# Two weight preparations in a fused FFT and gated MLP: first blocks taken in groups, projections in one PSUM bank each

## The chip, the cores and the metric

The kernel runs on one core of a Trainium2 chip. The metric is the device time of one execution in microseconds (us); lower is better. PE is TensorE (PEld its weight loads), DVE VectorE, ACT ScalarE, POOL GpSimd, SP the engine that only issues transfers.

## The reference

```
X = fft(x, axis=1); X = fft(X, axis=2).real      # x: 4 x 3008 x 256
h = X.reshape(12032, 256) @ w_in                 # 256 x 2048
g = h / (1 + exp(-h))
out = g @ w_out                                  # 2048 x 256, 12032 rows
```

[...]

## The kernel before

**What is computed where.** The transform over the 256 columns is folded into `w_in`: a cosine and sine table (`dft_sb`) is multiplied with each block of `w_in`, and the product is the left operand of the first layer. The transform over the 3008 rows is a matmul of folded rows of `x` with tables (`t2`, `te`, `to`). Its result is cut into 16 chunks (four classes in each of four batches) of about 376 columns. Each chunk runs against 16 blocks of 128 hidden columns, so the main loop has 256 steps (c, f). Every product is made from high and low parts in `float32r` (`uvh` and `uvl`, `abh` and `abl`, `gh` and `gl`, `woh` and `wol`), three matmuls for one.

**A step.** `first(c, f)` issues 6 matmuls of the first layer into a tile `pq` (two buffers of two PSUM banks). `act` lets DVE add a rank-one row (`ub` times `a128`, L349) and form sum and difference (L353, L354), then ACT makes Silu into `h` (L360) and the high part `gh` (L361). `rest` of the step before lets DVE subtract for the low part `gl` (L369). `second` of three steps earlier (LAG = 3) issues 12 matmuls into four accumulators `acc` (L380, L381, L385). In chunk 0 the first DIRECT = 8 steps take another way: 12 matmuls with a negated copy `vneg` give sum and difference at once (L332), there is no DVE work between PE and Silu, and the row `a128` and `ub` aren't needed.

**The beginning.** `w_in` comes in eight blocks of 256 columns. `load_w` loads one (SP, three buffers `win`), `ahead` starts `to_f32` with an absolute value on ACT (L76), `run(conv.pop(q))` finishes it with four DVE operations (L78, L80, L82, L84) into `wf` (two buffers), `project` multiplies with the table on PE (L441), `large` takes row 0 out on ACT (`row`, L446), sends it through a transfer to `a128` (L447, issued by ACT) and makes `abh` (L450), and `small` makes `abl` on DVE (L454). The projection has a tile of two banks, from a pool `ps` of two buffers, for blocks 1 and 3 from `pq`. Blocks 0 to 3 are done ahead of the main loop, between the folding of the first rows of `x` (`first_sums`, L167 to L173, once for 64 rows of `x2` and once for 128 rows of `x1`), the operand of chunk 0 (L213 to L220, `xh` L251, `xl` L264), its transform on PE (L280) and `spread`, which makes `row`, `ub` (a transfer, L312), `uvh`, `uvl` and `vneg`. Blocks 4 to 7 are finished inside steps 0, 1 and 2 (`late_w`, L513). The rows of `x` come as a load by SP and a second load by POOL that adds to it (L134).

**The second weight.** `w_out` comes in eight blocks too, two loaded by POOL at the start, the others by SP (L95) when the block two earlier has been read. `convert_all_wo` is a generator with four pulls a block: the same conversion, then `woh` on ACT (L101) and `wol` on POOL (L102). `act` pulls it in chunk 0: three times a step in the direct steps, once in the others.

**What sets the order.** Nothing reorders: each engine executes its instructions as the code emits them. Buffers are rings: a tile of a tag waits until the readers of the tile that held the buffer are done. The tag `half` has three buffers, shared by `row`, the `wf` of `w_out`, and parts of the folding. After step 2 the pools `wr` and `ps` are closed, and their place goes to the accumulators and the tables `te` and `to`.

## Time and profile before

| | before |
|---|---|
| median of 3 runs | 944.23 us (944.03 to 945.05) |
| profiled execution, its own time | 944.83 us |
| span of the profiled execution | 942.9 us |
| mean granted clock of PE | 0.975 |
| busy: PE, DVE, ACT, POOL | 887.7, 748.0, 534.3, 183.9 us |

The span is what lies between the first and the last instruction in the trace; the execution's own time is 1.9 us longer. A granted clock of 1.00 is 2.4 GHz, 0.50 is 1.2 GHz. Busy time of PE is modelled from pipelined matmuls, so a window in which PE is busy throughout says that it never waited long, and the count of matmuls in it says how fast it went.

### The profile page before, as it was taken

What the parts mean: (1) busy time and instruction counts of PE and PEld (TensorE: products, weight loads), DVE (VectorE), ACT (ScalarE), POOL (GpSimd) and SP (SyncE); (2) the same over time, 40 slices, a digit from 0 to 9 for tenths busy, and PEclk for the clock granted to TensorE, in tenths of its full rate; (3) what the DMA queues carried; (4) which work ended last, traced back from release to release, by engine and by line L of the source; (5) the groups of instructions that cost most, each with busy time, mean ns of one, the idle gap of its engine ahead of it and who ended that gap; (6) DMA issues with size and microseconds to landing.
All of it is one profiled execution on the core that took longest, in us unless ns stands there. A gap on an engine that the chain in (4) does not pass through costs nothing.

```text
span 942.9 us, 12965 instructions
## 1 busy us (share of the span) xinstructions
PE 887.7 (94%) x5056; PEld 879.2 (93%) x5056; DVE 748.0 (79%) x1199; ACT 534.3 (57%) x736; POOL 183.9 (20%) x212
## 2 busy tenths in 40 slices
PE   2455999999999999999999999999999999999998
PEld 1344999999999999999999999999999999999998
DVE  4534888799787979798887979798887978798785
ACT  1332657665556756475564646475654646465554
POOL 1000415329013205236030105230010101010000
PEclk8766999999999999999999999999999999999999
DMA  9510251160302027020302024020302020020300
GB/s 283 104 53 31 90 107 56 20 134 1 42 1 9 34 19 201 3 40 1 42 1 9 33 21 111 3 40 1 42 1 9 33 9 34 4 39 1 43 1 33
DMA packets 19453, 40.96 MB, mean 43 GB/s; under 512 B 3264, under 2 KB 13504, under 8 KB 17472
## 3 DMA queue, kind: packets, MB, share of 16 engines
q1 hardware_dynamic: 16352, 28.87, 16.6%
q0 software_dynamic: 1600, 10.81, 4.8%
q10 hardware_dynamic: 1440, 0.46, 0.8%
q8 instruction: 39, 0.64, 0.3%
q14 instruction: 22, 0.18, 0.1%
HBM read 24.70 MB, written 12.34 MB: 39 GB/s over the span
## 4 chain that ended last, share of the span: by engine, by line
PE 87%; DVE 6%; ACT 3%; DMA 1%; issue 1%; ACTq 0%; POOL 0%; DVEq 0%
PE acc L385 18%; PE acc L381 18%; PE acc L380 18%; PE pq L336 9%; PE pq L337 9%; PE pq L338 8%; PE pq L280 5%; PE pw L441 2%; PE pq L332 2%; DMA raw<-in_x_dram 1%; DVE gl L369 1%; DVE wf L84 1%; DVE wf L82 1%; PE pq L441 1%; ACT h L360 1%
## 5 line engine op out<-in xcount | busy, mean ns | idle before, releaser
L360 ACT ACTIVATE h<-h 128x752 f32<-128x752 f32 (+2 forms) x250 | 207.3, 829 | 290.9 <-DVE h L354 288.4
L381 PE MATMUL acc<-gh,wol 128*128 128x376 f32 (+1 forms) x1024 | 342.8, 335 | 0.0
L380 PE MATMUL acc<-gh,woh 128*128 128x376 f32 (+1 forms) x1024 | 342.3, 334 | 0.0
L369 DVE TENSOR_TENSOR gl<-h,gh 128x752 fp32r<-128x752 f32 (+2 forms) x258 | 254.9, 988 | 3.5 <-ACT gh L361 3.3
L385 PE MATMUL acc<-gl,woh 128*128 128x376 f32 (+1 forms) x1024 | 226.3, 335 | 0.0
L361 ACT ACTIVATE gh<-h 128x752 fp32r<-128x752 f32 (+2 forms) x258 | 214.2, 830 | 8.2
L349 DVE SCALAR_TENSOR_TENSOR h<-ub,a,pq 128x376 f32<-128x376 f32 (+1 forms) x248 | 150.0, 605 | 56.7 <-PE pq L338 54.8
L381 PEld LDWEIGHTS acc<-gh,wol 128*128 128x128 f32 x1024 | 192.7, 188 | 0.0
L380 PEld LDWEIGHTS acc<-gh,woh 128*128 128x128 f32 x1024 | 192.5, 188 | 0.0
L385 PEld LDWEIGHTS acc<-gl,woh 128*128 128x128 f32 x1024 | 181.2, 189 | 0.0
L336 PE MATMUL pq<-uvh,abh 128*128 128x376 f32 (+1 forms) x496 | 166.6, 336 | 0.0
L337 PE MATMUL pq<-uvl,abh 128*128 128x376 f32 (+1 forms) x496 | 166.2, 335 | 0.0
L338 PE MATMUL pq<-uvh,abl 128*128 128x376 f32 (+1 forms) x496 | 166.0, 335 | 0.0
L354 DVE TENSOR_TENSOR h<-h,pq 128x376 f32<-128x376 f32 (+1 forms) x248 | 135.7, 547 | 8.5
L353 DVE TENSOR_TENSOR h<-h,pq 128x376 f32<-128x376 f32 (+1 forms) x248 | 135.6, 547 | 8.3
L258 POOL TENSOR_TENSOR xl<-xf,xh 128x256 fp32r<-128x256 f32 x53 | 49.1, 950 | 382.0 <-ACT xh L251 190.9
L338 PEld LDWEIGHTS pq<-uvh,abl 128*128 128x128 f32 x496 | 93.6, 189 | 0.0
L337 PEld LDWEIGHTS pq<-uvl,abh 128*128 128x128 f32 x496 | 93.5, 189 | 0.0
L336 PEld LDWEIGHTS pq<-uvh,abh 128*128 128x128 f32 x496 | 93.4, 188 | 0.1
L441 PE MATMUL pw<-wf,dft_sb 128*128 128x256 f32 x48 | 22.2, 644 | 43.1 <-DVE wf L84 43.1
L441 PEld LDWEIGHTS pw<-wf,dft_sb 128*128 128x128 f32 x48 | 15.1, 329 | 48.3 <-DVE wf L84 29.5
L314 DVE TENSOR_TENSOR uvl<-pq,uvh 128x752 fp32r<-128x752 f32 (+1 forms) x16 | 15.1, 943 | 55.4 <-ACT uvh L313 55.4
(99 smaller groups left out, 541.4 us busy)
## 6 DMA issues: line engine op xcount, KB each, us to landing
out_dram<-o SPq DMA_DIRECT2D x48, 188.0 KB, 2.2
raw<-in_x_dram SPq DMA_DIRECT2D x5, 1024.0 KB, 11.4
raw<-in_x_dram POOLq DMA_DIRECT2D x5, 1024.0 KB, 8.1
win<-in_w_in_dram SPq DMA_DIRECT2D x8, 512.0 KB, 7.9
wo<-in_w_out_dram SPq DMA_DIRECT2D x6, 512.0 KB, 3.6
out_dram<-o SPq DMA_DIRECT2D x16, 189.0 KB, 2.2
ub<-row SPq DMA_DIRECT2D x11, 188.0 KB, 8.5
t<-in_t_dram POOLq DMA_DIRECT2D x1, 1128.0 KB, 13.5
```

The costliest lines, as they stand in the source:

```text
L336: nc.tensor.matmul(po, abh[:, i, fs], uvh[:, i, :n], start=True, stop=False)
L337: nc.tensor.matmul(po, abh[:, i, fs], uvl[:, i, :n], start=False, stop=False)
L338: nc.tensor.matmul(po, abl[:, i, fs], uvh[:, i, :n], start=False, stop=True)
L349: stt(p[:, :n], ub[:, :n], a128[f // 2][:, f % 2:f % 2 + 1], pq[:, 0, :n], op0=ALU.mult, op1=ALU.add)
L353: tt(h[:, 0, :n], p[:, :n], pq[:, 1, :n], op=ALU.add)
L354: tt(h[:, 1, :n], p[:, :n], pq[:, 1, :n], op=ALU.subtract)
L360: nc.scalar.activation(h[:, sg, :n], (pq if direct else h)[:, sg, :n], AF.Silu)
L361: nc.scalar.activation(gh[:, sg, :n], h[:, sg, :n], AF.Copy)
L369: tt(gl[:, sg, :n], g[:, sg, :n], gh[:, sg, :n].bitcast(F32), op=ALU.subtract)
L380: nc.tensor.matmul(po, wo[0][f // 2][:, f % 2, es], gh[:, sg, :n], start=f == 0, stop=False)
L381: nc.tensor.matmul(po, wo[1][f // 2][:, f % 2, es], gh[:, sg, :n], start=False, stop=False)
L385: nc.tensor.matmul(accs[c][i][:, :n], wo[0][f // 2][:, f % 2, es], gl[:, sg, :n], start=False, stop=f == NF - 1)
```

## The change

- **The order at the beginning.** Blocks 0, 1 and 2 of `w_in` are started one after the other (`ahead`, then `convert`, which is the rest of the conversion and the projection) before the first folding; blocks 5 and 6 likewise, around the transform. Blocks 0 to 6 are projected before step 0. Only `large(6)`, `project(7)` (step 0), `small(6)`, `large(7)` and `small(7)` (step 1) remain in the loop. `late_w` is gone, and the pools are closed after step 1.
- **Buffers.** A projection has a tile of one bank (two halves of 256 columns), four buffers in `ps`, none from `pq`. `win` has five buffers in place of three. `wf` of `w_in` comes from the ring `half` of three buffers, which `row` of `spread` and the `wf` of `w_out` share. The row for `a128` has a place of its own for each block (`rows`) in place of a buffer of `half`.
- **Queues.** The transfers to `a128` and the first `ub` are issued by SP, no longer by ACT. The load of `w_in` block 0 goes ahead of the rows of `x`, and blocks 1 and 2 go ahead of the 128 rows of `x1`.
- **Direct steps.** 6 in place of 8, so block 3 gets the extra ACT copy that zeroes its row 0, and the tables `te` and `to` are loaded at step 6.
- **`w_out`.** Loads run three blocks ahead in place of two; every third block has a buffer in the pool `tabs`. The absolute value of a block is emitted between the second and third DVE operation of the block before. The pulls are 2 in steps 0 and 1, 3 in steps 2 to 4, 2 in steps 5 to 15.
- **Later.** In chunk 1 the operand of chunk 2 is queued at step 8 in place of 10, and POOL's budget there is 1.3 in place of 1.1.

```diff
-DIRECT = 8
+DIRECT = 6
 def load_wo(q, queue=nc.sync):
-        wo_raw[q] = fold_p.tile([128, 2, D], I64, tag="ri0", name="wo", bufs=2)
+        wo_raw[q] = (tabs_p.tile([128, 2, D], I64, tag="wo", name="wo") if q % 3 == 2 else
+                     fold_p.tile([128, 2, D], I64, tag="ri0", name="wo", bufs=2))
 def convert_all_wo():
         for q in range(NF // 2):
+            for _ in range(2):
+                next(work)
+                yield
+            if q + 1 < NF // 2:
+                following = convert_wo(q + 1)
+                next(following)
             yield from work
-            if q + 2 < NF // 2:
-                load_wo(q + 2)
-            if q + 1 < NF // 2:
-                work = convert_wo(q + 1)
-                next(work)
+            if q + 3 < NF // 2:
+                load_wo(q + 3)
+            work = following
             yield
 def spread(c, po):
-        (nc.sync if c else nc.scalar).dma_start(out=ub[:, :n], in_=...)
+        nc.sync.dma_start(out=ub[:, :n], in_=...)
-    ps = late.enter_context(tc.tile_pool(name="ps", bufs=2, space=PSUM))
+    ps = late.enter_context(tc.tile_pool(name="ps", bufs=4, space=PSUM))
+    rows = wr.tile([128, 2, 128, 2], F32, name="rows")
 def load_w(q):
-        win[q] = wr.tile([128, 2, 256], I64, tag="win", name="win", bufs=3)
+        win[q] = wr.tile([128, 2, 256], I64, tag="win", name="win", bufs=5)
 def ahead(q):
-        wf32[q] = wr.tile([128, 2, 256], F32, tag="wf", name="wf", bufs=2)
+        wf32[q] = fold_p.tile([128, 2, 256], F32, tag="half", name="wf", bufs=3)
 def project(q):
-        pw = pws[q] = pq_tile() if q in (1, 3) else ps.tile([128, 2, 512], F32, tag="ps", name="pw")
+        pw = pws[q] = ps.tile([128, 2, 256], F32, tag="ps", name="pw")
 def large(q):
-        row = fold_p.tile([1, 128, 2], F32, tag="half", name="row", bufs=3)
+        row = rows[32 * (q % 4):32 * (q % 4) + 1, q // 4]
-        nc.scalar.dma_start(out=a128[q], in_=row)
+        nc.sync.dma_start(out=a128[q], in_=row)
...
+    load_w(0)
     load_x(1, 0, lo)
-    load_w(0)
+    load_w(1)
+    load_w(2)
     load_x(0, 0)
...
+    def convert(q):
+        run(conv.pop(q))
+        project(q)
     ahead(0)
+    ahead(1)
+    convert(0)
+    ahead(2)
+    convert(1)
     large(0)
+    convert(2)
+    ahead(3)
+    large(1)
+    small(0)
     run(first_sums(1, lo))
+    small(1)
+    large(2)
+    convert(3)
+    ahead(4)
+    small(2)
     run(first_sums(0))
...
+    large(3)
+    ahead(5)
+    ahead(6)
+    convert(4)
+    small(3)
     run(op)
     po = pq_tile()
+    run(conv.pop(5))
     transform(0, po)
+    project(5)
+    large(4)
+    convert(6)
     spread(0, po)
+    ahead(7)
+    small(4)
+    large(5)
+    run(conv.pop(7))
+    small(5)
...
+        if n == 0:
+            large(6)
+            project(7)
+        elif n == 1:
+            small(6)
+            large(7)
...
-            act(c, f, (3 if f < DIRECT else 1) * (wo_work,) if c == 0 else ())
-        if n < LAG:
-            for q in ((4, 5), (6,), (7,))[n]:
-                late_w(q)
-        if n == LAG - 1:
+            act(c, f, (2 + (1 < f < 5)) * (wo_work,) if c == 0 else ())
+        if n == 1:
+            small(7)
             late.close()
...
+            load_wo(2)
```

Three places of the built order follow, each before and then after. First DVE at the very beginning, from its fifth instruction on (the four before it are the conversion of block 0 in both). Before:

```order
L167 TENSOR_TENSOR raw<-raw 64x8x127
L169 SCALAR_TENSOR_TENSOR raw<-raw 64x8x127
L171 TENSOR_TENSOR sm<-raw 64x4x129
L173 TENSOR_TENSOR sm<-raw 64x4x127
L454 TENSOR_TENSOR abl<-pw,abh 128x2x256
L78 TENSOR_SCALAR wf<-wf 128x512
```

After:

```order
L78 TENSOR_SCALAR wf<-wf 128x512
L80 TENSOR_SCALAR wf<-wf 128x512
L82 SCALAR_TENSOR_TENSOR wf<-win,wf 128x512
L84 SCALAR_TENSOR_TENSOR wf<-win,wf 128x512
L78 TENSOR_SCALAR wf<-wf 128x512
L80 TENSOR_SCALAR wf<-wf 128x512
L82 SCALAR_TENSOR_TENSOR wf<-win,wf 128x512
L84 SCALAR_TENSOR_TENSOR wf<-win,wf 128x512
L460 TENSOR_TENSOR abl<-pw,abh 128x2x256
L172 TENSOR_TENSOR raw<-raw 64x8x127
```

Blocks 1 and 2 of `w_in` moved ahead of `abl` of block 0 and of the folding. The second place is ACT around the first Silu (`h<-pq`). Before:

```order
L450 ACTIVATE abh<-pq 128x2x256
L76 ACTIVATE wf<-wo 128x512
L360 ACTIVATE h<-pq 128x2x376
L361 ACTIVATE gh<-h 128x2x376
L446 ACTIVATE row<-pw 1x256
L447 DMA a_4_81<-row 128x1x2
L449 ACTIVATE pw<-zero 1x256
L450 ACTIVATE abh<-pw 128x2x256
L76 ACTIVATE wf<-win 128x512
```

After:

```order
L452 ACTIVATE rows<-pw 1x256
L455 ACTIVATE pw<-zero 1x256
L456 ACTIVATE abh<-pw 128x2x256
L76 ACTIVATE wf<-wo 128x512
L365 ACTIVATE h<-pq 128x2x376
L366 ACTIVATE gh<-h 128x2x376
L452 ACTIVATE rows<-pw 1x256
L455 ACTIVATE pw<-zero 1x256
L456 ACTIVATE abh<-pw 128x2x256
```

The absolute value of `w_out` block 0 stands ahead of the first Silu in both; around it stand blocks 3 and 4 of `w_in` before, and blocks 6 and 7 after. The third place is DVE in two steps of chunk 0 that are no longer direct. Before:

```order
L369 TENSOR_TENSOR gl<-h,gh 128x2x376
L349 SCALAR_TENSOR_TENSOR h<-ub,a_5_82,pq 128x376
L82 SCALAR_TENSOR_TENSOR wf<-wo,wf 128x512
L353 TENSOR_TENSOR h<-h,pq 128x376
L354 TENSOR_TENSOR h<-h,pq 128x376
L369 TENSOR_TENSOR gl<-h,gh 128x2x376
L349 SCALAR_TENSOR_TENSOR h<-ub,a_5_82,pq 128x376
L84 SCALAR_TENSOR_TENSOR wf<-wo,wf 128x512
L353 TENSOR_TENSOR h<-h,pq 128x376
L354 TENSOR_TENSOR h<-h,pq 128x376
```

After:

```order
L354 SCALAR_TENSOR_TENSOR h<-ub,a_4_81,pq 128x376
L84 SCALAR_TENSOR_TENSOR wf<-wo,wf 128x512
L358 TENSOR_TENSOR h<-h,pq 128x376
L359 TENSOR_TENSOR h<-h,pq 128x376
L78 TENSOR_SCALAR wf<-wf 128x512
L374 TENSOR_TENSOR gl<-h,gh 128x2x376
L354 SCALAR_TENSOR_TENSOR h<-ub,a_4_81,pq 128x376
L80 TENSOR_SCALAR wf<-wf 128x512
L358 TENSOR_TENSOR h<-h,pq 128x376
L359 TENSOR_TENSOR h<-h,pq 128x376
L82 SCALAR_TENSOR_TENSOR wf<-wo,wf 128x512
```

Between the four operations of a step stood one operation of the `w_out` conversion, and two stand there now.

## Rows read from the trace of the kernel before

**Rows 1.** Windows: us, then busy us (xinstructions) by engine, PEclk, DMA, GB/s.
```profile
62.90:76.30 13.40, 6.87 (x23) 5.90 (x21) 6.18 (x10) 4.60 (x8) 1.26 (x1) 0.63 0.14 40
130.00:190.00 60.00, 59.82 (x351) 59.51 (x350) 49.83 (x79) 40.70 (x65) 19.67 (x25) 1.00 0.25 36
240.00:440.00 200.00, 200.00 (x1168) 200.00 (x1168) 172.53 (x275) 124.74 (x172) 61.49 (x69) 1.00 0.24 41
```
**Rows 2.** Waits of PE over the span: releaser: us in total, times, longest.
```profile
PE pw L441 <- DVE wf L84: 43.1, 6, 10.5
```
**Rows 3.** Timeline, block 5 to block 6: start us, us, engine, line, operation.
```profile
59.79 3.78 PE L441 MATMUL pw<-wf,dft_sb 128*128 128x256 f32 x8 [6.57 <-DVE wf L84]
...
64.01 0.48 ACTq L447 DMA_DIRECT2D a<-row  x1
...
65.57 0.69 DVE L454 TENSOR_TENSOR abl<-pw,abh 128x512 fp32r<-128x512 f32 x1 [5.83 <-ACT abh L450]
...
72.44 0.69 DVE L84 SCALAR_TENSOR_TENSOR wf<-win,wf 128x512 uint32<-128x512 uint32 x1
...
73.27 3.38 PE L441 MATMUL pw<-wf,dft_sb 128*128 128x256 f32 x8 [6.53 <-DVE wf L84]
```
**Rows 4.** Timeline, conversion and projection of block 0.
```profile
7.45 0.66 ACT L76 ACTIVATE wf<-win 128x512 f32<-128x512 f32 x1 [4.78 <-DMA win<-in_w_in_dram]
8.14 0.43 DVE L78 TENSOR_SCALAR wf<-wf 128x512 f32<-128x512 f32 x1 [8.14 <-ACT wf L76]
...
10.54 3.78 PE L441 MATMUL pw<-wf,dft_sb 128*128 128x256 f32 x8 [10.54 <-DVE wf L84]
```
**Rows 5.** Transfers issued at 2 to 5 us, last by POOL: KB, us to landing.
```profile
raw<-in_x_dram SPq DMA_DIRECT2D x1, 1024.0 KB, 7.9
win<-in_w_in_dram SPq DMA_DIRECT2D x1, 512.0 KB, 8.8
win<-in_w_in_dram SPq DMA_DIRECT2D x1, 512.0 KB, 13.4
raw<-in_x_dram POOLq DMA_DIRECT2D x1, 1024.0 KB, 10.4
```
**Rows 6.** Timeline, folding of the 128 rows, operand and transform of chunk 0.
```profile
21.11 1.21 DVE L167 TENSOR_TENSOR raw<-raw 128x1016 f32<-128x1016 f32 x1
...
24.09 0.68 DVE L173 TENSOR_TENSOR sm<-raw 128x508 f32<-128x508 f32 x1
...
27.23 0.42 DVE L213 TENSOR_TENSOR xf<-sm 128x258 f32<-128x258 f32 x1
...
28.97 0.43 DVE L78 TENSOR_SCALAR wf<-wf 128x512 f32<-128x512 f32 x1
...
37.11 1.19 PE L280 MATMUL pq<-t,xl 128*128 128x376 f32 x6
```
**Rows 7.** The row of chunk 0, ACT behind it (timeline), and all transfers to `ub`.
```profile
38.34 0.47 ACT L311 ACTIVATE row<-pq 1x376 f32<-1x376 f32 x1 [1.08 <-PE pq L280]
...
43.25 0.65 ACT L76 ACTIVATE wf<-wo 128x512 f32<-128x512 f32 x1
...
DMA to landing us min/median/max: 8.5/8.6/9.5
```
**Rows 8.** First second-layer matmul (timeline); Silu group and `w_out` loads by SP (page).
```profile
93.94 0.33 PE L380 MATMUL acc<-gh,woh 128*128 128x376 f32 x1
L360 ACT ACTIVATE h<-h 128x752 f32<-128x752 f32 (+2 forms) x250 | 207.3, 829 | 290.9 <-DVE h L354 288.4
wo<-in_w_out_dram SPq DMA_DIRECT2D x6, 512.0 KB, 3.6
```
**Rows 9.** Timeline, low parts on DVE one step apart, and one beside POOL.
```profile
119.86 0.94 DVE L369 TENSOR_TENSOR gl<-h,gh 128x752 fp32r<-128x752 f32 x1
...
122.86 0.94 DVE L369 TENSOR_TENSOR gl<-h,gh 128x752 fp32r<-128x752 f32 x1
...
125.67 1.30 POOL L102 TENSOR_TENSOR wol<-wf,woh 128x512 fp32r<-128x512 f32 x1 [5.87 <-ACT woh L101]
125.87 1.89 DVE L369 TENSOR_TENSOR gl<-h,gh 128x752 fp32r<-128x752 f32 x1
```

More of the change, by code (lines that the diff above doesn't have):

```diff
@@ L311, in spread @@
         nc.scalar.activation(row[:, :n], po[0:1, 1, :n], AF.Copy)
-        (nc.sync if c else nc.scalar).dma_start(out=ub[:, :n], in_=row[:, :n].unsqueeze(0).to_broadcast([1, 128, n]))
+        nc.sync.dma_start(out=ub[:, :n], in_=row[:, :n].unsqueeze(0).to_broadcast([1, 128, n]))
         nc.scalar.activation(uvh[:, :, :n], po[:, :, :n], AF.Copy)
@@ L472, in fft_mlp @@
     load_wo(1, nc.gpsimd)
-    for q in range(1, 8):
+    for q in range(3, 8):
         load_w(q)
@@ L476, in fft_mlp @@
     nc.sync.dma_start(out=rot_sb[1], in_=rot2)
+    def convert(q):
+        run(conv.pop(q))
+        project(q)
     ahead(0)
-    run(conv.pop(0))
-    project(0)
+    ahead(1)
+    convert(0)
+    ahead(2)
+    convert(1)
     large(0)
+    convert(2)
+    ahead(3)
+    large(1)
+    small(0)
     run(first_sums(1, lo))
-    small(0)
-    ahead(1)
-    run(conv.pop(1))
-    project(1)
-    ahead(2)
-    large(1)
+    small(1)
[3 more added lines that the diff above has]
+    small(2)
     run(first_sums(0))
-    small(1)
     op = operand(0)
@@ L493, in fft_mlp @@
         next(op)
-    run(conv.pop(2))
-    project(2)
-    ahead(3)
+    large(3)
[3 more added lines that the diff above has]
+    small(3)
     run(op)
-    large(2)
-    small(2)
     po = pq_tile()
+    run(conv.pop(5))
     transform(0, po)
-    run(conv.pop(3))
-    project(3)
-    ahead(4)
+    project(5)
+    large(4)
+    convert(6)
     spread(0, po)
-    large(3)
-    small(3)
-    run(conv.pop(4))
-    project(4)
-    wo_work = convert_all_wo()
-    def late_w(q):
-        if q > 4:
-            run(conv.pop(q))
-            project(q)
-        large(q)
-        if q < 7:
-            ahead(q + 1)
-        small(q)
+    ahead(7)
[3 more added lines that the diff above has]
+    small(5)
+    wo_work = convert_all_wo()
     steps = [(c, f) for c in range(4 * B) for f in range(NF)]
@@ L531, in fft_mlp @@
     for c in range(4 * B - 1):
-        at(c, {1: 10, 3: 6}.get(c, 0), add, queue, ("op", c + 1), operand(c + 1))
+        at(c, {1: 8, 3: 6}.get(c, 0), add, queue, ("op", c + 1), operand(c + 1))
     at(1, 0, add, pool_queue, ("t2d", 0), fold_diffs(1, 0, lo))
@@ L590, in fft_mlp @@
             drain(queue, 0.6)
-            drain(pool_queue, 1.1 if c == 1 else 0.6)
+            drain(pool_queue, 1.3 if c == 1 else 0.6)
 def _rows(s):
```

## The prediction

> **What bounds the kernel now.** I read the windows first. From 240 to 440 us PE is busy throughout, at granted clock 1.00, and completes 1168 matmuls in 200 us, 0.1712 us each; from 130 to 190 us, where DVE and ACT are at their fullest, it is 351 in 60 us, the same rate [rows 1]. So from the first second-layer matmul, at 93.94 us [rows 8], to the end the kernel is a stream of matmuls, and only their number or a new stall changes that stretch. Ahead of it PE is half idle and at half clock: in 62.90:76.30 it is busy 6.87 of 13.40 us at 0.63 [rows 1]. The waits name the cause: projections wait 43.1 us in six waits for the last conversion operation on DVE [rows 2]. The timeline shows the loop behind it: block 5 is projected at 59.79 us, its `abl` is made at 65.57, only then comes the rest of the next block's conversion (72.44), and block 6 is projected at 73.27 [rows 3]. One block goes round PE, ACT, DVE and PE in 13.48 us, and in that time no engine is full. The question is when the stream begins if the blocks are no longer taken round one at a time.
>
> **Where the stream would begin.** The stream needs `gl` and `wol` of its first step, the accumulators' banks (free when `abl` of block 7 is made) and four `first`. I follow the new order.
>
> Loads. The folding of the 128 rows waits for a load of 1 MB and POOL's adding load. Before, the load was issued at about 2.0 us and landed 7.9 later, at 9.9; the adding load took 10.4 [rows 5] and so ended at about 20.6. Now two blocks of 512 KB stand ahead. The two behind it before took 8.8 and 13.4 us from about 2.5 and 3.0 [rows 5], so landed at 11.3 and 16.4: 1.4 and 5.1 us apiece, the second one while POOL's adding load ran. Two blocks cost 2.8 to 10.2 us. I take 5, nearer the low end, since little of POOL's traffic is there so early: the rows are complete at 25.6 us (23.4 to 30.8). Blocks 0 to 2 run through DVE and PE ahead of that, at 2.4 us each from L78 to the matmul [rows 4], with the first folding and block 3, and are done by then.
>
> To the transform. The folding takes 21.11 to 24.77, 3.7 us, and the operand 27.23 to 28.97, 1.7 us [rows 6]: 31.0. Then PE's order asks for block 4: conversion 2.4 us [rows 4], projection 3.78 us at the low clock [rows 3]: 37.2. The transform is 18 matmuls; six took 1.19 us [rows 6], so 3.6: 40.8 us. Blocks 5 and 6 convert on DVE beside it.
>
> **A new wait.** `spread` now writes `row` in 0.47 us [rows 7] and SP sends it to `ub`. That transfer takes 8.6 us to land, 8.5 to 9.5 over all of them [rows 7]: 49.9 us. The `wf` of `w_out` block 0 gets the buffer of the ring `half` that `row` had, because `wf` of `w_in` now takes places in that ring. So ACT's absolute value for that block must wait until `ub` has been read out, and the first Silu, `gh`, row 7 and `abh` of block 7 stand behind it on ACT, and on DVE the two operations for `z` and `abl` of blocks 6 and 7. Before, the ring turned otherwise: ACT made that absolute value at 43.25, 4.4 us after `row` was done, with the transfer still under way [rows 7]. PE has cover for most of it: three projections (3.38 us for one that began at the low clock [rows 3], less at the high one) and two `first` of 12 x 0.1712 = 2.05 us last till 50 to 54.
>
> After the wait: absolute value 0.66 [rows 4], 50.6. DVE then does four conversion operations, 2.3 us [rows 4], and three of about 0.69 [rows 3] between them: 54.9. `woh`, priced like an absolute value at 0.66, then Silu of step 1 at 0.83 [rows 8]: 56.4. This frees the `pq` buffer for `first(0, 3)`, 2.05 us: the stream begins at **58.5 us**. The next thing late is `w_out` block 2: SP issues it behind block 3, which waits for the last conversion operation at 54.9, so at about 55.9, and it lands 3.6 later [rows 8]; absolute value and Silu end at 61.0, and `first(0, 4)` could have begun at 60.55. That is 0.45 us: 59.0 us in effect. Against 93.94 the beginning gains **34.9 us**.
>
> **The other parts.** Two steps with 6 matmuls less: 12 x 0.1712 = **2.05 us** less on PE, which is the bound there. SP instead of ACT issuing the small transfers frees 0.48 us of ACT a block [rows 3]; it is in the chain only through the sums above, and costs nothing on SP, which has only loads in that time. One bank per projection removes the use of `pq`, so `first` and the projections no longer take buffers from each other; nothing else reads it. The one added ACT copy (block 3) and the moved operand of chunk 2 I cost at nothing: ACT is busy 40.70 of 60 us [rows 1] where the second lies.
>
> **What DVE pays.** The `w_out` conversion now falls on steps 6 to 14, two operations a step where one stood. A step with one lasts 3.00 us from `gl` to `gl` [rows 9], PE's step 18 x 0.1712 = 3.08. A second operation adds 2.3 / 4 = 0.57 [rows 4], so DVE falls behind by 0.49 a step. Beside POOL's `wol` a `gl` took 1.89 in place of 0.94 [rows 9], once a block, so 0.48 a step more at most: 0.97. From step 6 to 11, six steps, that is 2.9 to 5.8 us. PE notices only when it wants the `pq` buffer back, 30 matmuls or 5.1 us after it was filled; DVE needs 3.00 less `gl`, 2.1 to 2.3 us, for it, so 2.9 us of lag are free. At step 12 a transform of 30 matmuls gives DVE time again. So PE stalls 0 to 2.9 us; I take the middle, **1.5 us lost**.
>
> A rule that speaks against the change: the Trainium skill, "SBUF — State Buffer", section "Who interferes with whom", says that a DVE instruction with two SBUF inputs and a GpSimd instruction that reads SBUF exclude each other, the later one being blocked until the first is finished. The trace agrees: `gl` began 0.2 us after `wol` and took 0.95 us longer, of the 1.1 us that `wol` still had to run [rows 9]. By that rule alone the loss would be up to 4 us, the second rival.
>
> **The sum.** 944.83 - 34.9 - 2.05 + 1.5 = 909.4 us by the profiled execution, which lies 0.6 above the median of the runs: **908.7 us** forecast. Its own range: rows of `x` at 23.4, no stall of DVE, no wait for block 2 give 904.5; the middle of the late cases 912.
>
> **The rivals.** (1) The loads set the pace: both blocks ahead of the rows cost 5.1 us each, the rows are complete at 30.8, and all behind shifts by 5.2: 914. For it: five `win` buffers put still more loads beside POOL's adding load. Against: the first of the two blocks landed after only 1.4 us. (2) DVE sets the pace in steps 6 to 14: each `wol` blocks a DVE operation for its full 1.30 us [rows 9], 0.65 a step, so 1.14 us a step; six steps less the free 2.9 lose 3.9, and 913 with what steps 13 and 14 add. For it is the row with 1.89; against, that most operations in a step read PSUM or miss POOL. (3) The change doesn't do what it says: ACT, in order, waits for late loads ahead of the rows it should take out, and a block still takes its 13.48 us. Then only the direct steps and 0.48 us of ACT for eight blocks are gained: 938. Against: blocks 1 and 2 are converted from loads that land ahead of the rows of `x`. (4) Slower: `w_out` blocks come too late in the stream. ACT's absolute value stands ahead of the Silu, so a late block stops PE. A load has three blocks less one, four steps or 12.3 us, to land; it took 3.6 [rows 8]. From 12.3 on each microsecond is lost in up to five loads, and from 19.9 us a load 38 us are gone and the kernel is at 946.7, slower than before; even in the full queue of the start a block took 13.4 [rows 5].
>
> One smaller cost is in the range alone: PE idles about 3 us ahead of `first(0, 3)`. Granted clock fell to 0.63 in the window with long pauses [rows 1]; at half clock that step takes 2.05 us more.
>
> **How the numbers follow.** Chances: forecast 0.68, (1) 0.14, (2) 0.12, (3) 0.03, (4) 0.01, and 0.02 that the stream begins still earlier. The range 904 to 916 takes in the forecast's own range and the first two rivals, with the clock. A measurement of this kernel can tell about 0.2% from no change; all cases but (4) are faster by more: faster 0.985, same 0.005, slower 0.01.
>
> **What would show it.** Right: the first second-layer matmul at 57 to 61 us; blocks 0 to 6 projected ahead of the first `first`; ACT idle for 5 us or more ahead of the absolute value of `w_out` block 0 with the transfer to `ub` as releaser; PE busy throughout from about 61 us but for 0 to 3 us of waits for `h` of DVE in steps 9 to 12; 12 matmuls fewer. Wrong: the folding of the 128 rows beginning after 28 us (1); PE waiting over 3 us in steps 6 to 14 (2); projections 13 us apart (3); ACT waiting for `wo` loads in steps 3 to 12 (4). The weakest terms are the landing of the rows of `x` and the lag of DVE.

## The result and the profile after

The changed kernel takes **911.5 us** (median of three executions; a fourth took 3053 us, at full granted clock and for no reason that the record shows, and is left out here as it is in the ratio). The kernel before takes 944.6 in the same runs: ratio 0.9649, 95% interval 0.9630 to 0.9668. The forecast was 908.7 with a range of 904 to 916. The span of the profiled execution is 909.2 us in place of 942.9. Line numbers from here on are those of the changed kernel, in which `first` is L337 and L341 to L343, `second` L385 to L390, the Silu L365, `gl` L374, the projection L447 and `wol` L103; an edit that adds lines moves them by a few. The "conversion" is that of the weights, which arrive as 64-bit numbers: the kernel reads them as pairs of 32-bit words and makes 32-bit floats of them.

The same three windows as in [rows 1], with the same columns (us, then busy us and instructions of PE, PEld, DVE, ACT, POOL; granted clock, DMA share, GB/s):

```profile
62.90:76.30 13.40, 13.40 (x79) 13.40 (x79) 13.30 (x15) 8.97 (x13) 9.34 (x11) 1.00 0.40 132
130.00:190.00 60.00, 60.00 (x349) 60.00 (x348) 52.32 (x83) 38.45 (x54) 23.91 (x24) 1.00 0.32 61
240.00:440.00 200.00, 200.00 (x1168) 200.00 (x1167) 170.40 (x273) 125.32 (x174) 63.43 (x71) 1.00 0.24 41
```

The later two are as before. The first, in which PE was half idle at clock 0.63, is now in the middle of the stream: PE is busy throughout at clock 1.00, and DVE has no room left beside it (13.30 of 13.40). The waits of PE over the span, beside [rows 2] (us in total, times, longest):

```profile
PE pw L447 <- DVE wf L84: 20.9, 5, 8.7
PE pq L337 <- ACT h L365: 3.9, 3, 2.4
PE pq L341 <- DVE h L359: 1.3, 3, 0.6
```

The second and third line are new. The first fell from 43.1 us, and by more than that: [rows 2] counts the projections into `pw`, and before two blocks were projected into `pq` and waited, too.

```profile
PE pq L441 <- DVE wf L84: 8.5, 2, 6.9
```

So the wait for the conversion was 51.6 us and is now 20.9. The projections on the timeline show why it fell; in [rows 3] two of them stood 13.48 us apart:

```profile
8.71 5.84 PE L447 MATMUL pw<-wf,dft_sb 128*128 128x256 f32 x16 [8.71 <-DVE wf L84]
14.81 1.99 PE L447 MATMUL pw<-wf,dft_sb 128*128 128x256 f32 x8 [0.25 <-DVE wf L84]
23.12 3.52 PE L447 MATMUL pw<-wf,dft_sb 128*128 128x256 f32 x8 [6.32 <-DVE wf L84]
31.92 3.75 PE L447 MATMUL pw<-wf,dft_sb 128*128 128x256 f32 x8 [5.27 <-DVE wf L84]
39.04 3.61 PE L447 MATMUL pw<-wf,dft_sb 128*128 128x256 f32 x16
45.09 1.97 PE L447 MATMUL pw<-wf,dft_sb 128*128 128x256 f32 x8 [0.38 <-DVE wf L84]
```

Sixteen matmuls are two blocks. All eight blocks are projected by 47.1 us; before, block 6 alone began at 73.27. The rows that answer to [rows 5] are the loads of the beginning (KB, median us to landing), and the one that answers to [rows 6] is the first folding operation on the 128 rows of `x`:

```profile
raw<-in_x_dram SPq DMA_DIRECT2D x1, 1024.0 KB, 9.8
raw<-in_x_dram POOLq DMA_DIRECT2D x1, 1024.0 KB, 10.5
...
24.10 1.22 DVE L172 TENSOR_TENSOR raw<-raw 128x1016 f32<-128x1016 f32 x1 [0.43 <-DMA raw<-in_x_dram]
```

The rows are complete at 24.1 us and their folding begins 3.0 later than before, since two blocks of `w_in` now go ahead of them. Then the place of the wait that the prediction announced, beside [rows 7] and [rows 8]: ACT takes the row out, waits for the transfer to `ub`, and the stream begins at 56.80.

```profile
39.24 0.47 ACT L316 ACTIVATE row<-pq 1x376 f32<-1x376 f32 x1 [2.12 <-PE pq L285]
...
48.53 0.66 ACT L76 ACTIVATE wf<-wo 128x512 f32<-128x512 f32 x1 [3.07 <-DMA ub<-row]
...
54.63 0.44 PE L337 MATMUL pq<-uvh,abh 128*128 128x376 f32 x1 [2.38 <-ACT h L365]
...
56.80 0.33 PE L385 MATMUL acc<-gh,woh 128*128 128x376 f32 x1
...
58.30 0.68 ACT L76 ACTIVATE wf<-wo 128x512 f32<-128x512 f32 x1 [2.85 <-DMA wo<-in_w_out_dram]
```

So the beginning gained 93.94 - 56.80 = 37.1 us, where the forecast had 35.4 (34.9 with its 0.45 for block 2 taken off), and yet the span fell by 33.7 alone. From the first second-layer matmul to the end there were 942.9 - 93.94 = 849.0 us before, and 909.2 - 56.80 = 852.4 after; with 12 matmuls fewer (2.05 us) it should have been 846.9. **5.5 us were lost in the stream**, where the forecast had 1.95. This sum is made for every kernel below, since it keeps the two halves apart:

| kernel | median us | ratio to before, 95% | stream begins | from there to the end | lost |
|---|---|---|---|---|---|
| before | 944.6 | | 93.94 | 849.0 | 0 |
| after | 911.46 | 0.9649 (0.9630 to 0.9668) | 56.80 | 852.4 | 5.5 |
| e1, row of its own | 908.45 | 0.9620 (0.9606 to 0.9633) | 54.22 | 852.4 | 5.5 |
| e2, no `wol` by POOL | 907.65 | 0.9610 (0.9597 to 0.9622) | 58.89 | 847.2 | 0.3 |
| e3, 8 direct steps | 910.79 | 0.9644 (0.9631 to 0.9657) | 58.58 | 851.1 | 2.1 |
| e4, before with 6 direct steps | 947.15 | 1.0029 (1.0018 to 1.0039) | 94.56 | 851.0 | 4.1 |
| e5, blocks one by one | 943.59 | 0.9990 (0.9981 to 1.0000) | 88.59 | 853.3 | 6.4 |
| e6, e1 and e3 together | 907.30 | 0.9605 (0.9591 to 0.9619) | 53.75 | 851.2 | 2.2 |
| e7, e6 with `wol` on DVE | 907.06 | 0.9600 (0.9586 to 0.9615) | 55.37 | 850.1 | 1.2 |
| e8, small transfers on ACT | 912.33 | 0.9656 (0.9640 to 0.9673) | 57.58 | 852.8 | 5.9 |
| e9, e6 with rows of `x` first | 910.05 | 0.9631 (0.9618 to 0.9644) | 56.80 | 851.1 | 2.1 |
| e10, e9 with `wol` 1 to 7 on DVE | 908.48 | 0.9613 (0.9600 to 0.9627) | 57.95 | 850.2 | 1.2 |
| e11, e6 with `wol` 1 to 7 on DVE | 906.13 | 0.9595 (0.9582 to 0.9608) | 54.24 | 850.1 | 1.1 |
| e12, e4 without `wol` by POOL | 945.23 | 1.0007 (0.9998 to 1.0016) | 92.36 | 851.1 | 4.2 |

"Lost" is measured against 849.0 us with 8 direct steps and 846.9 with 6. The last three columns are of one profiled execution each, and its beginning differs from one execution to the next: with the same order of loads the folding of the 128 rows began between 24.1 us (after) and 25.9 (e3). The median and the columns therefore agree within about 2 us, and the lost time is the steadier of the two: kernels with the same stream show the same loss within 0.4. It isn't free of the beginning, though, as e2 shows below. The kernel before took 944.5 to 944.8 in all rounds of runs.

### The profile page after: what moved, and what is told of

Same layout as the page of the kernel before. It is cut to its first block, busy times and chain, and to the rows that moved or that the text cites. A ratio compares the mean times of both kernels' runs of the same rounds, so it can differ in the third digit from the quotient of the medians.

```text
span 909.2 us, 12939 instructions
## 1 busy us (share of the span) xinstructions
PE 877.7 (97%) x5044; PEld 869.1 (96%) x5044; DVE 752.6 (83%) x1205; ACT 535.5 (59%) x737; POOL 185.7 (20%) x212
## 4 chain that ended last, share of the span: by engine, by line
PE 87%; DVE 7%; DMA 3%; issue 1%; ACT 1%; SPq 0%; DVEq 0%; ACTq 0%
PE acc L386 18%; PE acc L390 18%; PE acc L385 18%; PE pq L341 9%; PE pq L342 9%; PE pq L343 9%; PE pq L285 5%; DMA raw<-in_x_dram 2%; DVE gl L374 2%; DMA ub<-row 1%; DVE wf L78 1%; DVE wf L82 1%; DVE h L354 1%; DVE h L359 1%; DVE h L358 1%
## 5 line engine op out<-in xcount | busy, mean ns | idle before, releaser
L365 ACT ACTIVATE h<-h 128x752 f32<-128x752 f32 (+2 forms) x252 | 209.0, 829 | 291.3 <-DVE h L359 288.6
L385 PE MATMUL acc<-gh,woh 128*128 128x376 f32 (+1 forms) x1024 | 342.5, 334 | 0.8 <-ACT o L398 0.8
L374 DVE TENSOR_TENSOR gl<-h,gh 128x752 fp32r<-128x752 f32 (+2 forms) x258 | 254.6, 987 | 3.2 <-ACT gh L366 3.0
L390 PE MATMUL acc<-gl,woh 128*128 128x376 f32 (+1 forms) x1024 | 226.3, 335 | 0.0
L354 DVE SCALAR_TENSOR_TENSOR h<-ub,a,pq 128x376 f32<-128x376 f32 (+1 forms) x250 | 151.0, 604 | 56.7 <-PE pq L343 54.7
L385 PEld LDWEIGHTS acc<-gh,woh 128*128 128x128 f32 x1024 | 192.5, 188 | 1.3 <-ACT o L398 1.1
L390 PEld LDWEIGHTS acc<-gl,woh 128*128 128x128 f32 x1024 | 181.2, 189 | 0.0
L341 PE MATMUL pq<-uvh,abh 128*128 128x376 f32 (+1 forms) x500 | 168.5, 337 | 1.7 <-DVE h L359 1.3
L343 PE MATMUL pq<-uvh,abl 128*128 128x376 f32 (+1 forms) x500 | 167.3, 335 | 0.0
L341 PEld LDWEIGHTS pq<-uvh,abh 128*128 128x128 f32 x500 | 94.1, 188 | 3.3 <-DVE h L359 2.6
L343 PEld LDWEIGHTS pq<-uvh,abl 128*128 128x128 f32 x500 | 94.4, 189 | 0.0
L205 POOL TENSOR_TENSOR ri<-ri,raw 128x256 f32<-128x256 f32 (+1 forms) x28 | 27.7, 998 | 84.9 <-ACT ri L201 84.5
L447 PE MATMUL pw<-wf,dft_sb 128*128 128x256 f32 x64 | 20.6, 481 | 21.0 <-DVE wf L84 20.9
```

The lines of the kernel that those rows point to most:

```text
L341: nc.tensor.matmul(po, abh[:, i, fs], uvh[:, i, :n], start=True, stop=False)
L343: nc.tensor.matmul(po, abl[:, i, fs], uvh[:, i, :n], start=False, stop=True)
L354: stt(p[:, :n], ub[:, :n], a128[f // 2][:, f % 2:f % 2 + 1], pq[:, 0, :n], op0=ALU.mult, op1=ALU.add)
L365: nc.scalar.activation(h[:, sg, :n], (pq if direct else h)[:, sg, :n], AF.Silu)
L374: tt(gl[:, sg, :n], g[:, sg, :n], gh[:, sg, :n].bitcast(F32), op=ALU.subtract)
L385: nc.tensor.matmul(po, wo[0][f // 2][:, f % 2, es], gh[:, sg, :n], start=f == 0, stop=False)
```

## The experiments

**What the gain is made of (e5).** The grouping alone is undone (several calls to a line here):

```
-    ahead(0); ahead(1); convert(0); ahead(2); convert(1); large(0); convert(2); ...
+    ahead(0); convert(0); large(0); run(first_sums(1, lo)); small(0); ahead(1); convert(1); ...
...
+        if n < LAG:
+            for q in ((4, 5), (6,), (7,))[n]:
+                late_w(q)          # [convert,] large, ahead of the next, small
```

> The changed kernel with the grouping alone undone: blocks 0 to 4 ahead of the main loop and 5 to 7 in its steps 0 to 2 go round one at a time in the order of the kernel before; the order of the loads, five win buffers, places for rows, one-bank projections, SP's queue for the small transfers and 6 direct steps stay. The steps with three pulls are 3 to 5 in place of 2 to 4, since block 2 of w_out is loaded a step later. Theory (the grouping is nearly the whole gain): a block still goes round PE, ACT, DVE and PE in 13.48 us less the 0.48 of the issue that ACT no longer has; the stream begins at about 88 to 92 us in place of 56.8, and the time is 938 to 943. Rival (the buffers, the queue and the earlier loads bring most of it, and the order little): projections 8 us apart or less, the stream begins before 75, and the time is 925 or less.

Measured: 943.59 us. The projections on the timeline stand 12 us apart again:

```profile
47.91 3.75 PE L447 MATMUL pw<-wf,dft_sb 128*128 128x256 f32 x8 [5.16 <-DVE wf L84]
60.01 3.75 PE L447 MATMUL pw<-wf,dft_sb 128*128 128x256 f32 x8 [6.11 <-DVE wf L84]
71.86 3.78 PE L447 MATMUL pw<-wf,dft_sb 128*128 128x256 f32 x8 [5.16 <-DVE wf L84]
...
88.59 0.44 PE L385 MATMUL acc<-gh,woh 128*128 128x376 f32 x1 [0.17 <-DVE abl L460]
```

The round of a block is 12.1 and 11.85 us in place of 13.48, so the buffers, the queue and the places for rows saved about 1.5 us a round. The stream begins at 88.59, inside the expected 88 to 92. The time lies 0.6 above the expected range, since this kernel loses 6.4 us in its stream. The grouping is worth 32.1 us, as good as the whole gain of 33.1; all the rest of the change together brought 1.1 us, at the edge of what the interval tells from nothing, beside a loss in the stream.

**The new wait (e1).** The row of chunk 0 gets a tile that nobody else wants at that time:

```
-        row = fold_p.tile([1, CH], F32, tag="half", name="row", bufs=3)
+        row = (fold_p.tile([1, CH], F32, tag="half", name="row", bufs=3) if c else
+               mp.tile([128, CH], F32, tag="o", name="o", bufs=4)[0:1])
```

> The changed kernel, with one edit: the row of chunk 0 gets a buffer of the output tiles (unused until chunk 0 ends) in place of a buffer of the ring that wf shares. Theory (the wait for ub is on the chain, and DVE is full from there to 112 us, so what DVE gets earlier the stream keeps): ACT's 3.1 us of waiting for ub and DVE's 3.7 us behind it go, the first second-layer matmul moves from 56.8 to about 53.3 us, the whole is 3.1 to 3.7 us shorter than 911.5: 907.8 to 908.4. Rival (the wait is hidden, or the time comes back as a longer lag of DVE in steps 6 to 14): 910.5 to 911.5.

Measured: 908.45 us, 3.0 less than after. The timeline of ACT and PE (its lines from L316 on are one higher):

```profile
45.94 0.68 ACT L76 ACTIVATE wf<-wo 128x512 f32<-128x512 f32 x1
...
54.22 0.34 PE L386 MATMUL acc<-gh,woh 128*128 128x376 f32 x1
```

The absolute value of `w_out` block 0 comes 2.6 us sooner and waits for nothing, and the stream begins 2.6 sooner. The loss in the stream is unchanged at 5.5. So the wait that shared buffers made is real, lies on the path, and cost 2.6 to 3.0 us. The stream was expected at about 53.3 and came 0.9 later; the time lies at the upper edge of its expected range.

**Who loses the time in the stream (e2).** POOL fills `wol` with zeros, so the low part of `w_out` is left out:

```
-        nc.gpsimd.tensor_tensor(wl, wf, wh.bitcast(F32), op=ALU.subtract)
+        nc.gpsimd.memset(wl.bitcast(F32), 0.0)
```

> The changed kernel, but POOL fills wol (the low part of w_out) with zeros instead of subtracting; the low part of w_out is left out of the product. POOL then writes and doesn't read in that place. Theory A (the stream's losses of 5.5 us come from POOL's reading instructions that hold up DVE): the L78 beside it fall from 1.35 to 0.43 us, gl and L82 from up to 2.03 and 1.79 to 0.94 and 0.69, and PE's waits in steps 6 to 15 (3.0 us) go; 3 to 5 us shorter: 906.5 to 908.5. Theory B (the number of DVE operations alone makes the lag): the durations may fall, the time by less than 1 us: 910.5 to 911.5.

Measured: 907.65 us, and the loss fell from 5.5 to 0.3 us. In after, the timeline has these pairs of POOL and DVE:

```profile
65.62 1.30 POOL L103 TENSOR_TENSOR wol<-wf,woh 128x512 fp32r<-128x512 f32 x1
65.69 2.03 DVE L374 TENSOR_TENSOR gl<-h,gh 128x752 fp32r<-128x752 f32 x1
...
81.05 1.28 POOL L103 TENSOR_TENSOR wol<-wf,woh 128x512 fp32r<-128x512 f32 x1 [3.27 <-ACT woh L102]
81.26 1.35 DVE L78 TENSOR_SCALAR wf<-wf 128x512 f32<-128x512 f32 x1
```

`gl` takes 2.03 us beside `wol` and 0.94 alone [rows 9], L78 1.35 beside and 0.43 alone [rows 4]: each is longer by about what `wol` still had to run. What that does to the pace is seen in the first DVE operation of each step, L354, of after at steps 7 and 11:

```profile
75.40 0.59 DVE L354 SCALAR_TENSOR_TENSOR h<-ub,a,pq 128x376 f32<-128x376 f32 x1
...
91.01 0.59 DVE L354 SCALAR_TENSOR_TENSOR h<-ub,a,pq 128x376 f32<-128x376 f32 x1
```

and of e2 at the same two steps:

```profile
75.72 0.59 DVE L354 SCALAR_TENSOR_TENSOR h<-ub,a,pq 128x376 f32<-128x376 f32 x1
...
89.12 0.60 DVE L354 SCALAR_TENSOR_TENSOR h<-ub,a,pq 128x376 f32<-128x376 f32 x1
```

Four steps take 15.61 us in after, 3.90 each, and 13.40 in e2, 3.35 each; PE needs 3.08. DVE is the bound of this stretch even without POOL, by 0.27 us a step, which PE's two buffers absorb; with POOL it is 0.82 a step, which they don't. The four steps differ by 2.21 us. The two `L78` beside `wol` (1.35 and 1.36) make 1.9 of them; the rest is two operations at 75.9 and 77.5 us that stand beside `xl`, which e2 has done by then. The first matmul of each `first` in after, and of the transform behind step 12, shows where it reaches PE (idle before it in brackets; in e2 these steps show none):

```profile
77.58 0.44 PE L341 MATMUL pq<-uvh,abh 128*128 128x376 f32 x1
...
81.40 0.44 PE L341 MATMUL pq<-uvh,abh 128*128 128x376 f32 x1 [0.45 <-DVE h L359]
...
85.41 0.45 PE L341 MATMUL pq<-uvh,abh 128*128 128x376 f32 x1 [0.64 <-DVE h L359]
...
89.02 0.44 PE L341 MATMUL pq<-uvh,abh 128*128 128x376 f32 x1 [0.23 <-DVE h L359]
...
93.03 0.74 PE L285 MATMUL pq<-te,xh 128*128 128x256 f32 x4 [0.65 <-DVE h L359]
```

From 77.58 on the starts are 3.82, 4.01, 3.61 and 4.01 us apart in place of 3.1. The brackets are smaller than that, since PE's busy time is modelled: the spacing of starts is the better measure. By it the 5.5 us lie in three places: 1.0 at the wait for block 2 of `w_out` (58.30 above), 4.0 between 75 and 102 us, where DVE sets the pace, and 1.1 at the change to chunk 1, where PE waits for the accumulators:

```profile
117.15 0.49 ACT L201 ACTIVATE ri<-raw,rot_sb 64x256 f32<-64x256 f32 x1
...
117.55 1.57 ACT L398 ACTIVATE o<-acc 128x376 f32<-128x376 f32 x4
...
118.06 0.44 PE L385 MATMUL acc<-gh,woh 128*128 128x378 f32 x1 [0.81 <-ACT o L398]
```

(Behind it the stream is 0.5 shorter than before.) ACT empties the accumulators (L398) behind two operations for later rows of `x` (L200 and L201); before, it emptied them first (150.43) and did those later (from 153.50). What brings them forward is POOL's raised budget in chunk 1. All kernels built on the changed one but e2 wait 0.6 to 0.8 us there, e11 too, whose DVE holds PE up nowhere. No run takes the budget back by itself, so how much of the 1.1 is its doing, and how much DVE's lag, isn't shown.

In e2 the three places come to 0, 0.9 and 0. So without POOL's reading 3.1 us of DVE's pace are won, and the 1.1 at the change of chunk go with them. The 1.0 at block 2 isn't cured in e2, only covered: the block came as late as ever (ACT waited for it until 59.08), but PE came to need it later. For e2's profiled stream began 2.1 us after that of after: 0.7 from the loads and the transform, and 1.3 from the clock. That is why its profiled execution gained 3.1 us and not 5.2; the median gained 3.8. In both kernels PE was idle for 2.3 to 2.4 us ahead of `first(0, 3)`; after it the granted clock was 1.00 in after and 0.57 in e2, by the windows of `first(0, 3)` in after, then in e2, and then in e3 (below), which had the same pause:

```profile
54.63:56.80 2.17, 2.17 (x12) 2.17 (x13) 2.12 (x6) 0.82 (x1) 1.20 (x1) 1.00 0.94 331
```

```profile
55.38:58.89 3.51, 3.51 (x12) 3.51 (x13) 3.40 (x10) 0.81 (x1) 0.00 (x0) 0.57 0.83 279
```

```profile
55.75:58.58 2.83, 2.83 (x13) 2.83 (x13) 2.75 (x7) 0.81 (x1) 1.20 (x1) 0.74 0.88 333
```

The same 12 matmuls took 2.17, 3.51 and 2.83 us.

**The direct steps (e3, e4).** e3 is the changed kernel with `DIRECT = 8`; e4 is the kernel before with `DIRECT = 6`, its three pulls kept in steps 0 to 7.

> The changed kernel with 8 direct steps again. 12 matmuls more on PE (2.05 us), 6 DVE operations (3.4 us) fewer in steps 6 and 7. Theory (DVE sets the pace in chunk 0): the lag shrinks by more than PE gains work, 0 to 1.5 us shorter than 911.5: 910 to 911.5, PE's waits for h of DVE under 1 us. Rival (PE is the bound there too): 2.05 us longer, 913.5.

> The kernel before with 6 direct steps and nothing else changed (the pulls of the w_out conversion stay at three up to step 7). Theory: 2.05 us less on PE; DVE gets 6 operations more and has three pulls in steps 6 and 7, which takes back 0 to 2 us: 942.5 to 944.5. Rival (the direct steps are what gave the gain of the change in part): more than 3 us shorter, under 941.

Measured: e3 910.79 us, 0.7 less than after in spite of 12 more matmuls; the intervals overlap, so all that can be said is that it is no slower. Its loss is 2.1 in place of 5.5 (0.9 of it the low clock, which lasted into the first second-layer matmuls and covered the wait for block 2), and at the first step that isn't direct DVE waits 1.86 us for PE, so it has caught up by then. e4 took 947.15, **slower** than before by 2.7, against an expected gain of up to 2. The window 112.4 to 130 us of before, and then of e4:

```profile
112.40:130.00 17.60, 17.60 (x109) 17.49 (x108) 17.39 (x28) 10.79 (x15) 6.64 (x7) 1.00 0.46 162
```

```profile
112.40:130.00 17.60, 14.86 (x83) 13.91 (x82) 17.39 (x29) 9.93 (x14) 6.17 (x8) 1.00 0.50 182
```

In this window DVE was busy for 17.39 of 17.60 us already before; PE then goes from 109 matmuls to 83. Each step less of the direct kind takes 6 matmuls (1.03 us) from PE and gives three operations to an engine that has no room for them there. So the expected 2.05 us were a gain on the engine that was the bound and a larger loss on the one next to it.

**Is it POOL in e4, too (e12)?** e4, and POOL's subtraction replaced by zeros as in e2 (the low part of `w_out` is left out).

> The kernel before with 6 direct steps, and POOL fills wol with zeros in place of the subtraction, so that the low part of w_out is left out. With the subtraction this kernel took 947.15 us, 2.7 more than the kernel before, and lost 4.1 us after the first second-layer matmul. Theory (POOL's reading is what makes DVE late): nearly all of the 4.1 us come back, 942.5 to 944.0. Rival (DVE's own work in steps 6 to 11 is too much, with POOL or without): 945.5 to 947.2.

Measured: 945.23 us, between the two expectations. The loss in the stream didn't move (4.2 against 4.1); what was gained lies ahead of the stream, which began 2.2 us sooner in this execution, for a reason that isn't shown. The theory falls for this kernel. The timeline of DVE has

```profile
102.55 0.97 DVE L78 TENSOR_SCALAR wf<-wf 128x512 f32<-128x512 f32 x1 [2.24 <-ACT wf L76]
103.55 1.75 DVE L80 TENSOR_SCALAR wf<-wf 128x512 uint32<-128x512 uint32 x1
105.23 1.46 DVE L369 TENSOR_TENSOR gl<-h,gh 128x752 fp32r<-128x752 f32 x1
...
107.13 2.33 DVE L82 SCALAR_TENSOR_TENSOR wf<-wo,wf 128x512 uint32<-128x512 uint32 x1
...
112.34 0.43 DVE L78 TENSOR_SCALAR wf<-wf 128x512 f32<-128x512 f32 x1 [1.25 <-ACT wf L76]
```

with 0.43, 0.43, 0.94, 0.69 and 0.43 alone: 4.0 us are still lost beside POOL's other work of that time, the low part of the next operand (`xl`, 0.73 to 1.32 us each), two transfers that POOL issues and memsets. Three conversion operations a step stand there too, where after has two. And DVE stood idle for 3.5 us more, in the brackets: in the order of before, ACT makes the absolute value of the next block only when the last operation of the block before is done, and DVE waits for it (1.26 and 1.25 us in e4, at 104.70 and 111.49). The changed kernel makes it two operations sooner, and its DVE has no such wait from 59 to 115 us. Which of the three is the largest part in e4 and e12 stays open.

**The small transfers (e8).** `a128` and the first `ub` are issued by ACT again:

```
-        nc.sync.dma_start(out=a128[q], in_=row)
+        nc.scalar.dma_start(out=a128[q], in_=row)
```

> The changed kernel with the small transfers (a128, and ub of chunk 0) issued by ACT again, as in the kernel before; all else as in the changed kernel. Theory (the issues lie in ACT's wait for ub, all but that of block 7): 0.2 to 0.8 us slower, 911.7 to 912.5. Rival (ACT's issue time of 0.48 us is in the chain with every block): five or more blocks, 913.9 to 915.8.

Measured: 912.33 us, 0.9 above after, within what the intervals leave open. ACT waits 1.48 us for `ub` there in place of 3.07: the issues lie in that wait. This part of the change is worth nothing measurable by itself in the new order.

**Two edits together (e6), and `wol` on DVE (e7).** e6 joins e1 and e3. e7 has DVE make `wol`, one pull later:

```
-        nc.gpsimd.tensor_tensor(wl, wf, wh.bitcast(F32), op=ALU.subtract)
+        lows[q] = lambda: tt(wl, wf, wh.bitcast(F32), op=ALU.subtract)
...
+                if i and q:
+                    lows.pop(q - 1)()
...
```

> The changed kernel with both single edits that gained: the row of chunk 0 in a tile of its own, and 8 direct steps. Theory (two separate causes, the wait for the transfer and the lag of DVE in steps 6 to 9): the gains of 3.25 and 0.9 us add, 907.5 us (907.0 to 908.0), the stream begins at 54.2, and the only long wait of PE in it is the one for block 2 of w_out, at ACT, 2.8 us. Rival (one hides the other: the earlier stream meets a late block 2 of w_out, and the direct steps gain nothing more): 908.3 to 908.7.

> As the kernel with the row of its own and 8 direct steps, but DVE makes wol, with the second operation of the next block, and POOL none. Theory (a subtraction of 128 x 512 on POOL costs DVE more than it would cost DVE to make it: a DVE operation beside it grew by 0.9 to 1.0 us, and gl, with 752 elements in place of 512, takes 0.94 on DVE, so wol some 0.65): DVE gets 0.3 us a block, in eight blocks 2.4; about half of it is on PE's path: 906.3 us (905.0 to 907.3). Rival (DVE is full and pays the whole 0.65 us a block, while the block by POOL lay mostly in DVE's pauses): PE waits longer for h, 908.5 to 911.

Measured: e6 907.30 and e7 907.06 us. In e6 both gains are there: the stream begins at 53.75 and loses 2.2. In e7 the loss falls to 1.2, since a `wol` on DVE takes 0.69 us against the 0.9 to 1.1 that POOL's cost it; but its stream begins 1.6 later, of which 1.1 came with later loads. The expected 906.3 wasn't reached, and 0.2 us between e6 and e7 is within the noise; the loss in the stream tells them apart, the time doesn't.

**The rows of `x` first (e9), and a mixed `wol` (e10, e11).** e9 is e6 with the loads in another order:

```
     load_x(1, 0, lo)
+    load_x(0, 0)
     load_w(1)
     load_w(2)
-    load_x(0, 0)
```

> The kernel with the row of its own and 8 direct steps, and the 128 rows of x loaded ahead of blocks 1 and 2 of w_in again. In the changed kernel the rows are issued at 3.4 us and land at 13.3, and POOL's adding load ends 10.5 later, at 24.1; in the kernel before they were issued at 2.0 and landed at 9.9. Theory (the beginning hangs on these rows alone: load, adding load, folding, operand, transform): the rows are complete at 20.5 to 22, the folding of the 128 rows and the first second-layer matmul (53.75) come 2 to 3.5 us earlier, and the time is 904.0 to 905.5. Rival (blocks 1 and 2, which then land at 11 to 17 us, stand ahead of the folding on DVE and hold it, or the adding load gets slower): the folding begins at 24 or later, and the time is 907 to 909.

> As the kernel with the rows of x ahead, and DVE makes wol of blocks 1 to 7, POOL that of block 0 alone, so that DVE has no more to do ahead of the stream. With wol of all blocks on DVE the stream began 1.6 us later (55.37 in place of 53.75; the rows of x were 1.1 us later there) and lost 1.1 us less. Theory: what is gained in the stream stays, and the start is that of the kernel with the rows ahead: 0.5 to 1.3 us faster than that one. Rival (the stream's rest of loss is the wait for block 2 of w_out, not POOL's): the same time within 0.3 us.

> The changed kernel with the row of its own, 8 direct steps, the loads in the changed kernel's order, and wol of blocks 1 to 7 on DVE, that of block 0 on POOL. Theory (the gains are separate: 1.6 us for wol, as between the two kernels with the rows of x ahead, and the start of the kernel without it, 53.75): 905.0 to 906.5 us. Rival (most of that 1.6 was chance of the start, since wol on DVE for all blocks had brought 0.2 here): 906.8 to 907.4.

Measured: e9 910.05 us, 2.75 more than e6: the direction of the rival, and 1 us above its range. ACT's absolute value of block 3 of `w_in`, which waits for its load, on the timeline of after and then of e9:

```profile
17.32 0.67 ACT L76 ACTIVATE wf<-win 128x512 f32<-128x512 f32 x1 [3.94 <-DMA win<-in_w_in_dram]
```

```profile
22.00 0.66 ACT L76 ACTIVATE wf<-win 128x512 f32<-128x512 f32 x1 [7.22 <-DMA win<-in_w_in_dram]
...
27.18 1.21 DVE L172 TENSOR_TENSOR raw<-raw 128x1016 f32<-128x1016 f32 x1
```

The load of block 3 stands at the same place in the queue, behind the same bytes, and landed 4.7 us later. What differs is that the rows of `x` land sooner, so that POOL's adding load, and the loads of `t2` and `w_out` that POOL issues behind it, begin 2.6 us sooner (10.96 in place of 13.57) and run beside block 3 for longer; that this is the cause is inferred. Block 3's conversion and `abl` of block 2 stand ahead of the folding on DVE, which begins at 27.2 in place of 24.5. So the order of the loads that the change chose was the better one, though it makes the rows of `x` later. e10 is e9 with `wol` of blocks 1 to 7 on DVE: 908.48, 1.6 less than e9 where 0.5 to 1.3 were expected; 0.9 of it is the smaller loss in the stream. e11 is the same with the loads of the changed kernel: **906.13 us** (ratio 0.9595, 0.9582 to 0.9608), inside the expected range and the fastest of all. DVE waits for PE at the first step that isn't direct, and PE for DVE nowhere in the stream:

```profile
74.98 0.61 DVE L364 SCALAR_TENSOR_TENSOR h<-ub,a,pq 128x376 f32<-128x376 f32 x1 [2.63 <-PE pq L353]
```

## Why the prediction was right, and which terms were off

The mechanism was right for the beginning: it moved by what the grouping gives, and e5 shows that nearly all of the gain is that. For the stream it was wrong that only the number of matmuls would change. The total lay 2.8 us too low. By the spans it is 1.8: 3.5 us more were lost in the stream, less the 1.7 by which it began sooner. The other 1.0 is the step from one execution to the median: the forecast took off the 0.6 by which the profiled execution of before lay above its median, and that of after lies 0.5 below. (The terms of the sum give 908.8 and not 908.7.) That two errors of opposite sign half cancelled is luck.

- **Rows of `x` at 25.6 us:** measured 24.1. The two blocks ahead of them cost 3.5 us and not 5 (24.1 less the 20.6 of the prediction); with it everything to the stream came 1.5 to 1.7 us sooner (transform's end 39.2 in place of 40.8).
- **The wait for `ub`:** forecast until 49.9, measured 48.53, 9.3 us after the row began, where 9.1 were forecast. ACT was idle for 3.07 us of it, not for 5: it had `vneg`, an absolute value and two blocks of `large` to do. e1 shows that the wait was on the path.
- **The stream begins at 58.5:** measured 56.80.
- **`w_out` block 2 late, 0.45 us:** it was about 1.0, by the start of the step after it (59.72 - 54.63 = 5.09 us in place of 24 x 0.1712 = 4.11, one step of `first` and `second`).
- **Two direct steps less, a gain of 2.05 us:** wrong in sign. It counted PE's matmuls alone. e3 and e4 show that the six DVE operations that come with it cost more: the time from the stream's beginning to the end got 1.3 us shorter with the 12 matmuls back (e3) and 2.1 longer without them (e4).
- **Lag of DVE, 1.5 us:** this is the term that failed; 4.0 of the 5.5 us lost belong to it. The pace was sized fairly: 3.57 a step without POOL and 4.05 with it were the bounds; 3.90 was measured in after, and 3.35 without `wol` in e2, 0.22 less than the lower bound. The free 2.9 us were wrong. They hold for a DVE that starts the stretch level with PE; but DVE had been full since the wait for `ub` ended (30.68 of 31 us from 59 to 90), and at step 6 it began 1.4 us after PE had filled the buffer. Half of the cover was used before the stretch began. The middle of a range was also taken where the row with 1.89 us pointed to its upper end. And the stretch where DVE is fullest was misread: 130 to 190 us has it busy for 83%, 240 to 440 us for 86% [rows 1], and the window from 112.4 to 130 shown under e4, just where the loss came, for 99%.
- **POOL's raised budget in chunk 1** has no term in the sum. It puts two operations ahead of ACT's emptying of the accumulators, where 1.1 us are lost in after, in part through it.
- **Rival (1)** didn't occur: the rows were complete at 24.1, not 30.8.
- **Rival (2), DVE sets the pace in steps 6 to 14,** is what the stream did, at 3.90 us a step where the rival had 4.22 (3.08 + 1.14). POOL's `wol` makes 0.55 of them by e2. The prediction cites the rule for this from the Trainium skill, "SBUF — State Buffer", section "Who interferes with whom". e2 bears it out: without POOL's subtraction `L78` and `gl` take 0.42 and 0.94 us from step 7 to step 11. The Trainium skill counts a DVE instruction with a single SBUF input there only where it runs in a two-port mode. The TENSOR_SCALAR of L78 has one input and grew from 0.43 to 1.35 us; its 0.43 us alone, where the two-input L82 takes 0.69 for as many elements, fit such a mode, and nothing else here shows it.
- **Rival (3),** that a block still takes its old round, is what e5 makes by hand: 943.6. **Rival (4)** didn't occur: ACT waited for a `w_out` load once.
- **The clock after PE's pause,** in the range alone, cost nothing in after, 1.3 us in e2 and 1.5 in e3.
- **The signs:** the stream began 0.2 us ahead of the 57 to 61 named, ACT was idle for 3.07 us where 5 were named, and PE's waits in steps 6 to 14 are 2.4 us by the brackets but 4.0 by the spacing, past the 3 that would speak for rival (2).

## What to carry to other kernels

Moving work from the engine that is the bound to its neighbour is a gain only for as long as the neighbour has room in that very stretch; before pricing it, read the neighbour's busy share there (17.39 of 17.60 us here), not over the span (748.0 of 942.9). Slack in buffers is to be counted from where the later engine stands when the stretch begins, not from zero. And where rings are shared, each new user of a ring has to be followed to the slowest reader of the buffer it gets: one `row` of 1.5 KB held up the first Silu by 2.6 us.

## What the runs showed of the hardware

A POOL subtraction of 128 x 512 from SBUF held up the DVE operation that ran into it by about its own rest (0.43 to 1.35 us, 0.94 to 2.03), and grew itself, from 1.30 to 2.07, where DVE had begun first:

```profile
61.51 0.94 DVE L374 TENSOR_TENSOR gl<-h,gh 128x752 fp32r<-128x752 f32 x1
...
61.55 2.07 POOL L103 TENSOR_TENSOR wol<-wf,woh 128x512 fp32r<-128x512 f32 x1 [5.72 <-ACT woh L102]
```

A transfer of 188 KB that repeats one row of 1.5 KB to 128 partitions took 8.5 to 9.5 us from issue to landing [rows 7], 8.5 to 9.1 in after, where 512 KB of `w_out` took 3.6 [rows 8]. And after a pause of PE of 2.3 to 2.4 us, with the same matmuls ahead of it, the mean granted clock of the next 12 matmuls was 1.00 in after, 0.74 in e3 and 0.57 in e2; what decides it isn't shown.
